# Row-wise scores issued ahead of each burst of narrow products, with three filling products between

## The chip, the cores and the metric

The kernel runs on one core of a Trainium2 chip. The metric is the time of one execution on the device in microseconds (us), the median of several runs. TensorE does the matmuls, ACT (the scalar engine) the exponentials, DVE (the vector engine) the reductions and most copies out of PSUM, POOL (GpSimd) sums between tiles in SBUF, and SP issues the DMAs.

## The reference

Two independent halves, put side by side in the last dimension, all in fp32:

```
A:  q = x @ wq  (32 heads of 32), k = x @ wk, v = x @ wv  (one key and value head for all)
    p = softmax(q k^T / sqrt(32)) for each head, over 2048 keys
    a = concat(p v) @ wo                                   x: [1, 2048, 1024]
B:  y = dft_seq_re @ (x @ dft_hid_re^T) - dft_seq_im @ (x @ dft_hid_im^T)
out = concat([a, y], axis=-1)                              [1, 2048, 2048]
```

## The kernel before

**Two kinds of work in one order.** The 32 heads in groups of four (8 groups) and the 2048 queries in blocks of 512 (4 blocks) make 32 *units* of attention. Everything else, projections, the transform of B in two stages and the output projection, is *fill*: groups of 24 matmuls (12 in the first stage of the transform), each group accumulating one bank of PSUM. Large operands are split into a high and a low part, and each product is made of three matmuls. `take(n)` issues n of these matmuls ("products" below); after each it runs `pump()`, which starts the loads, sums, casts and stores that fall due by the count of fill (`pos["fill"]`).

**Attention by steps.** A unit has SU = 32 steps, so there are 1024 in all. In the main loop step n does two different things for two different units:

- `score_step(n + SU + LEAD)`, 44 steps ahead: `scores(s)` computes 128 queries against 1024 keys (two matmuls into `pss`, two buffers of two banks each), DVE takes the row maximum `nm`; `row_sums(s - 1)` lets ACT take exponentials of the step before, in place, with their row sum. These give each row's maximum and sum. Some steps later `lse_1` to `lse_4` join the halves; `lse_3` transposes them on TensorE (`ident`), and they go into the operands of the next part.
- `expo(n)`: the column-wise scores, 128 keys against two heads' 512 queries (two matmuls into `pst`, which has one buffer of two banks), from which ACT writes the exponentials `p`.

**The burst.** After every eighth step `pv` multiplies the exponentials of the eight steps before with v: 16 narrow products of 32 columns each, one after the other, into one of the two banks that the fill uses too (`psb`); then DVE copies or adds the bank to `ov`. Ahead of a burst and of the transposition `aside()` issues up to five more products where a group of fill has just begun or is about to end. `bank` hands out the two banks in turn.

**What sets the order.** Each engine's instructions keep the program's order. `level(n + 1)` at the end of a step issues as much fill as is owed by then; fill issued by `aside` counts, so the next `level` issues less. PRO = 494 products lie ahead of the loop, FILL = 5472 is the total, and LAST = 24 are held back. Before the change the share of a block of eight steps goes evenly to the seven steps that have no burst:

```
def level(n):
    x = (n // 8 + max(n % 8 - 1, 0) / 7) / (total // 8)
    take(int((FILL - PRO - LAST) * x) + PRO - pos["fill"])
```

In the profile nearly all instructions have the line of the helper that records them (L66), so one goes by tile names: `psb<-rh,mh`, `psb<-rl,mh` and `psb<-rh,ml` are fill, `pss` row-wise scores, `pst` column-wise scores, `psb<-p,v` the burst, `psb<-ident` the transposition.

Of the kernel before, what the change touches and what calls it, by code (L numbers as in the profile page):

```python
# [87 lines left out]
def tile_kernel(ctx: ExitStack, tc, xT, wq, wkv, wo, xbT, wT, cT, out):  # L88
# [50 lines left out]
    class Line:  # L139
# [22 lines left out]
        def pump(self):  # L162
            for k in range(4):
                while self.may(k) and self.items[self.n[k]].due - self.lead[k] <= pos["fill"]:
                    self.step(k)
# [6 lines left out]
    pos = {"fill": 0, "s": 0}  # L172
# [128 lines left out]
    def at(p, f):  # L301
        k = len(later)
        while k and later[k - 1][0] > p:
            k -= 1
        later.insert(k, (p, f))

    def run_later():
        while later and later[0][0] <= pos["fill"]:
            later.pop(0)[1]()
# [8 lines left out]
    def store(to, of, key=None):  # L318
        def go():
            move(sp, to, of)  # L320
            if key:
                ready.add(key)
        soon(go)
# [4 lines left out]
    def bank(name, open_=False):  # L328

        b = 1 - cur["bank"] if cur["bank"] is not None else int(used[1] < used[0])  # L330
        cur["at"] += 1
        used[b] = cur["at"]
        if open_:
            cur["bank"] = b
        return ps_b[b].tile([P, W], F32, name=name)
# [10 lines left out]
    def product(g, ps, j):  # L346
        c, w = divmod(j, 3)
        l, r = g.left[c // 4], g.right[c]
        a = (l.lo if w == 2 else l.hi)[:, c % 4]
        te.matmul(ps[:g.rows], a, r.lo if w == 1 else r.hi, start=j == 0, stop=j == g.n - 1)  # L350

    def take(n):
        for _ in range(n):
            if cur["group"] >= len(groups):
                return
            g = groups[cur["group"]]
            j = pos["fill"] - g.at
            if j == 0:
                cur["ps"] = bank("psb", True)
            if j % 3 == 0:  # L360
                RL.force(g.right[j // 3])
            if j % 12 == 0:
                ML.force(g.left[j // 12])
            product(g, cur["ps"], j)
            pos["fill"] += 1
            if j == g.n - 1:
                cur["group"] += 1
                assert all(hasattr(it, "done") for it in g.ys)
                g.post(cur["ps"])
                cur["at"] += 1  # L370
                used[cur["bank"]] = cur["at"]
                cur["bank"] = None
                if g.ys:
                    at(pos["fill"] + 2 * BEHIND, lambda n=len(g.ys): yused.__setitem__(0, yused[0] + n))
            pump()
            run_later()

    def aside():

        if cur["group"] >= len(groups):  # L380
            return
        g = groups[cur["group"]]
        j = pos["fill"] - g.at
        if 0 < j < 6:
            take(6 - j)
        elif j > g.n - 6:
            take(g.n - j)
# [152 lines left out]
    def wo_set(e):  # L540
        return [Item([(lambda g=g: wo[g * P:(g + 1) * P, e * W:(e + 1) * W], 1)]) for g in range(NG)]
# [40 lines left out]
    SU = 32  # L582
    LEAD = 12
    total = SU * len(units)
# [3 lines left out]
    def open_unit(u):  # L588
        b, g = units[u]
        assert ("q", b, g) in ready  # L590
        q = qsp.tile([P, 4, W], F32R, name="qst")
        gp.memset(q[96:P].bitcast(F32), 0.0)
        for r, src in enumerate((qh_d, ql_d, qh_d)):
            move(sp, q[r * DH:(r + 1) * DH], src[b][g].rearrange("(h d) c -> d h c", d=DH))
        qst[u] = q
        nm[u] = sm.tile([P, 2, NC], F32, name="nm")
        ls[u] = sm.tile([P, 2, NC], F32, name="ls")

    def scores(s):
        u, r = divmod(s, SU)  # L600
        i, j = divmod(r, 2)
        h, t = divmod(i, 4)
        ps = ps_s.tile([P, 2 * W], F32, name="pss")
        for a in range(2):
            k0 = (2 * j + a) * W
            te.matmul(ps[:, a * W:(a + 1) * W], qst[u][:, h, t * P:(t + 1) * P], kst[:, k0:k0 + W], start=True, stop=True)
        dve.tensor_reduce(nm[u][:, j, i:i + 1], ps, axis=AX.X, op=ALU.max, negate=True)
        pend[s] = ps

    def row_sums(s):  # L610
        if s not in pend:
            return
        ps = pend.pop(s)
        u, r = divmod(s, SU)
        i, j = divmod(r, 2)
        act.activation(ps, ps, AF.Exp, bias=nm[u][:, j, i:i + 1], accum_out=ls[u][:, j, i:i + 1])

    def lse_1(u):
        m = sm.tile([P, NC], F32, name="mm")
        d = sm.tile([P, 2, NC], F32, name="md")  # L620
        dve.tensor_tensor(m, nm[u][:, 0], nm[u][:, 1], op=ALU.min)
        for j in range(2):
            dve.tensor_sub(d[:, j], m, nm[u][:, j])
        lse[u] = m, d

    def lse_1b(u):
        act.activation(lse[u][1], lse[u][1], AF.Exp)

    def lse_2(u):
        m, d = lse[u]  # L630
        l = sm.tile([P, NC], F32, name="l")
        m2 = sm.tile([P, 3, NC], F32, name="m2")
        dve.tensor_mul(d, d, ls[u])
        dve.tensor_add(l, d[:, 0], d[:, 1])
        dve.tensor_copy(m2[:, 0].bitcast(F32R), m)
        dve.tensor_sub(m2[:, 1], m, m2[:, 0])
        dve.reciprocal(m2[:, 2], l)
        lse[u] = m2

    def lse_3(u):  # L640
        m2 = lse.pop(u)
        aside()
        pm = bank("psb")
        te.transpose(pm[:3 * NC, :P], m2.rearrange("p a b -> p (a b)"), ident)
        mt = sm.tile([3 * NC, P], F32, name="mt")
        dve.tensor_copy(mt, pm[:3 * NC, :P])
        cur["at"] += 1
        lse[u] = mt

    def lse_4(u):  # L650
        mt = lse.pop(u)
        for a in range(2):
            move(sp, qst[u][96 + a:97 + a].rearrange("o h (t c) -> o (h t) c", c=P), mt[a * NC:(a + 1) * NC])
        sp.dma_start(r_d[u], mt[2 * NC:])
# [16 lines left out]
    def pv(u, k):  # L671

        aside()
        ps = bank("psb")
        for c in range(4 * k, 4 * k + 4):
            for h in range(4):
                te.matmul(ps[h * DH:(h + 1) * DH], v[:, c], pt[u, c, h // 2][:, h % 2], start=c == 4 * k, stop=c == 4 * k + 3)
        if k == 0:
            ov[u] = onp.tile([P, W], F32, name="ov")
            dve.tensor_copy(ov[u], ps)  # L680
        else:
            dve.tensor_add(ov[u], ov[u], ps)
        cur["at"] += 1
        if k == NC // 4 - 1:
            b, g = units[u]
            hi_ = onp.tile([P, W], F32R, name="oh")
            lo_ = onp.tile([P, W], F32R, name="ol")
            lse["out"] = hi_, lo_

            def low():  # L690
                dve.tensor_sub(lo_, ov[u], hi_.bitcast(F32))
                if u + 1 < len(units):
                    store(oh_d[b][g], hi_)
                    store(ol_d[b][g], lo_, ("o", b, g))

            ends.append(lambda: dve.tensor_mul(ov[u], ov[u], rb[u]))
            ends.append(lambda: dve.tensor_copy(hi_, ov[u]))
            ends.append(low)

    def score_step(s):  # L700

        if s < total:
            u, r = divmod(s, SU)
            if r == SU - 6 and u + 1 < len(units):
                open_unit(u + 1)
            scores(s)
        row_sums(s - 1)
        u, e = divmod(s - SU, SU)
        if 0 <= u < len(units):
            if e == 1:  # L710
                lse_1(u)
            elif e == 2:
                lse_1b(u)
            elif e == 3:
                lse_2(u)
            elif e == 5:
                lse_3(u)
            elif e == 7:
                lse_4(u)
# [17 lines left out]
    PRO = pos["fill"]  # L737
    FILL = end[0]
    LAST = 24


    def level(n):
        x = (n // 8 + max(n % 8 - 1, 0) / 7) / (total // 8)
        take(int((FILL - PRO - LAST) * x) + PRO - pos["fill"])

    for n in range(total):
        u, r = divmod(n, SU)
        if n == total - 12:
            w1 = wo_set(1)
            add([o_group(NQ - 1, t, e, ws) for e, ws in ((0, w0), (1, w1)) for t in range(4)])  # L750
        score_step(n + SU + LEAD)
        if ends:
            ends.pop(0)()
        expo(n)
        if r == 16:
            inverse(u)
        if r % 8 == 0 and n:
            pv(*divmod(n // 8 - 1, 4))
        level(n + 1)

# [71 lines left out]
```

## Time and profile before

| | |
|---|---|
| median of 3 runs | 2856.29 us (2856.1 to 2858.78) |
| the profiled execution | 2857.77 us, its span 2856.0 us |
| granted TensorE clock, mean | 0.998 |
| busy share: TensorE, its weight loads, ACT, DVE, POOL | 98%, 67%, 79%, 65%, 42% |
| first and last `pst` matmul | 161.4 and 2794.9 us |
| DMA over the span | 167 GB/s |

The span runs from the first instruction to the last. Busy times of matmuls overlap, and their ends are modelled; starts are what to go by. In rows of the timeline the columns are start, duration (us), engine, line, operation, out<-in, shapes, count of merged instructions and, in brackets, the idle time before it and what ended that. PE is TensorE's matmuls, PEld its weight loads.

### The profile page before, as it was taken

The numbers are of one execution on the slowest core, as the hardware profiler recorded it, in microseconds if no ns is written. First come the engines' busy times: TensorE is split into PE (matmuls) and PEld (weight loads), VectorE is DVE, ScalarE is ACT, GpSimd is POOL, SyncE is SP. The second block draws the span as 40 slices with busy tenths as digits, with TensorE's granted clock in tenths as the row PEclk, the third lists the DMA queues.
The fourth block names the chain that finished last, engine by engine and source line by source line (L and its number), as shares of the span: only waits on it lengthen the run. The fifth ranks groups of instructions, "written<-read, shape, count | busy, mean of one in ns | idle before, by whom it ended". The sixth has DMA issues, their size and how long they took to land.

```text
span 2856.0 us, 40040 instructions
## 1 busy us (share of the span) xinstructions
PE 2798.5 (98%) x13904; PEld 1923.4 (67%) x13904; DVE 1869.8 (65%) x2295; ACT 2242.7 (79%) x3286; POOL 1211.7 (42%) x928
## 2 busy tenths in 40 slices
PE   8999999999999999999999999999999999999999
PEld 5776666767666666766666667666666666666656
DVE  5766666767777777666776676776776676755410
ACT  4688888878788888888788878778888788888751
POOL 1211123554424336555564454775766653520000
PEclk9999999999999999999999999999999999999999
DMA  8965435766576455454452454564555533554445
GB/s 296 297 191 171 148 101 166 236 211 198 186 232 209 164 176 162 148 169 127 150 188 92 126 166 123 178 202 144 174 166 152 180 120 99 163 151 137 126 141 170
DMA packets 315723, 480.84 MB, mean 168 GB/s; under 512 B 33408, under 2 KB 98432, under 8 KB 315520
## 3 DMA queue, kind: packets, MB, share of 16 engines
q1 hardware_dynamic: 315520, 478.28, 53.6%
q8 instruction: 109, 1.79, 0.3%
q14 instruction: 94, 0.77, 0.1%
HBM read 364.12 MB, written 112.98 MB: 167 GB/s over the span
## 4 chain that ended last, share of the span: by engine, by line
PE 84%; DVE 6%; ACT 4%; issue 2%; DMA 2%; POOL 1%; SPq 1%; ACTq 0%; POOLq 0%; DVEq 0%
PE psb L66 53%; PE pst L66 16%; PE pss L66 15%; ACT p L66 2%; DVE nm L66 2%; ACT pss L66 1%; DVE mh L66 1%; DMA r<-s 1%; SPq L66 1%; DVE ov L66 1%; DVE rh L66 1%; POOL m L66 1%; POOL ml L66 0%; DVE md L66 0%; DMA p<-in_xT_dram 0%
## 5 line engine op out<-in xcount | busy, mean ns | idle before, releaser
L66 DVE TENSOR_REDUCE nm<-pss 128x1 f32<-128x1024 f32 x1024 | 1248.6, 1221 | 441.7 <-PE pss L66 439.1
L66 ACT ACTIVATE p<-pst 128x1024 f32<-128x1024 f32 x1024 | 1054.5, 1030 | 401.0 <-PE pst L66 394.0
L66 ACT ACTIVATE pss<-pss,nm 128x1024 f32<-128x1024 f32 x1024 | 1118.2, 1092 | 105.8 <-DVE nm L66 99.0
L66 PE MATMUL psb<-rh,mh 128*128 128x512 f32 (+1 forms) x1852 | 730.6, 394 | 9.6 <-ACT rh L66 7.8
L66 PE MATMUL psb<-rh,ml 128*128 128x512 f32 (+1 forms) x1852 | 730.0, 394 | 0.7 <-POOL ml L66 0.7
L66 PE MATMUL psb<-rl,mh 128*128 128x512 f32 (+1 forms) x1852 | 729.5, 394 | 0.3 <-DVE rl L66 0.3
L66 PE MATMUL pst<-qst,kst 128*128 128x512 f32 x2048 | 662.4, 404 | 22.1 <-ACT p L66 21.1
L66 PE MATMUL pss<-kst,qst 128*128 128x512 f32 x2048 | 657.3, 402 | 10.3 <-ACT pss L66 10.1
L66 POOL TENSOR_TENSOR ml<-m,mh 128x512 fp32r<-128x512 f32 x292 | 383.0, 1312 | 503.1 <-DVE mh L66 272.1
L66 POOL TENSOR_TENSOR rl<-r,rh 128x512 fp32r<-128x512 f32 x214 | 280.8, 1312 | 728.1 <-DVE rh L66 463.7
L66 PEld LDWEIGHTS pss<-kst,qst 128*128 128x128 f32 x2048 | 373.5, 188 | 198.8 <-issue 93.1
L66 PEld LDWEIGHTS pst<-qst,kst 128*128 128x128 f32 x2048 | 367.1, 188 | 161.8 <-ACT p L66 84.3
L66 PE MATMUL psb<-p,v 128*32 128x512 f32 x4096 | 466.0, 595 | 1.7 <-DVE y L66 1.7
L66 PEld LDWEIGHTS psb<-rh,mh 128*128 128x128 f32 (+1 forms) x1852 | 347.1, 187 | 94.9 <-ACT rh L66 8.3
L66 PEld LDWEIGHTS psb<-rl,mh 128*128 128x128 f32 (+1 forms) x1852 | 347.0, 187 | 84.4 <-DVE rl L66 1.5
L66 PEld LDWEIGHTS psb<-rh,ml 128*128 128x128 f32 (+1 forms) x1852 | 347.1, 187 | 84.3 <-POOL ml L66 1.1
L66 PEld LDWEIGHTS psb<-p,v 128*32 128x32 f32 x4096 | 120.0, 109 | 277.7 <-issue 263.8
L66 DVE TENSOR_TENSOR ov<-ov,psb 128x512 f32<-128x512 f32 x96 | 65.9, 686 | 297.6 <-PE psb L66 297.5
L66 POOL TENSOR_TENSOR m<-m,m 128x512 f32<-128x512 f32 x192 | 254.0, 1323 | 12.0 <-DMA m<-in_cT_dram 7.0
L66 POOL TENSOR_TENSOR r<-r,r 128x512 f32<-128x512 f32 x112 | 148.5, 1326 | 221.9 <-DMA r<-in_wT_dram 109.1
L66 ACT ACTIVATION_READ_ACCUMULATOR pss<-pss,nm 128x1 f32 x1024 | 214.3, 209 | 0.0
L66 DVE CAST mh<-m 128x512 fp32r<-128x512 f32 x291 | 178.4, 613 | 20.5 <-POOL m L66 11.4
(66 smaller groups left out, 828.5 us busy)
## 6 DMA issues: line engine op xcount, KB each, us to landing
m<-in_cT_dram SPq DMA_DIRECT2D x384, 256.0 KB, 3.7
r<-s SPq DMA_DIRECT2D x192, 256.0 KB, 4.4
y<-y SPq DMA_DIRECT2D x96, 256.0 KB, 4.5
r<-in_wT_dram SPq DMA_DIRECT2D x80, 256.0 KB, 4.3
m<-in_xbT_dram SPq DMA_DIRECT2D x80, 256.0 KB, 4.6
y<-u SPq DMA_DIRECT2D x80, 256.0 KB, 3.0
qst<-qh SPq DMA_DIRECT2D x64, 256.0 KB, 5.8
s<-y SPq DMA_DIRECT2D x64, 256.0 KB, 2.9
```

What stands on the lines that cost most here:

```text
L66: return lambda *a, **k: self.tc.keep_in_program_order(f(*a, **k))
```

## The change

In every step with a burst (n a multiple of 8, not 0), after `expo(n)`, three products of fill are issued, then the row-wise scores of the next step (s = n + 45) with the row sums of the present one; then comes the burst. The following step finds its scores already asked for and only issues the row sums of them. `level` is rewritten to the new order: of a block's share (w products) the burst's step has three, the step behind it half of what each of the other six has. The opening of a unit stays tied to its step.

```diff
-    def score_step(s):
-
-        if s < total:
+    asked = [0]
+
+    def ask(s):
+
+        if s < total and s == asked[0]:
+            asked[0] += 1
             u, r = divmod(s, SU)
             if r == SU - 6 and u + 1 < len(units):
                 open_unit(u + 1)
             scores(s)
-        row_sums(s - 1)
+            row_sums(s - 1)
+        else:
+            row_sums(min(s, total - 1))
+
+    def score_step(s):
+
+        ask(s)
         u, e = divmod(s - SU, SU)
...
     def level(n):
-        x = (n // 8 + max(n % 8 - 1, 0) / 7) / (total // 8)
-        take(int((FILL - PRO - LAST) * x) + PRO - pos["fill"])
+        w = (FILL - PRO - LAST) / (total // 8)
+        m = n % 8
+        take(int(w * (n // 8) + (3 + (w - 3) * max(m - 1.5, 0) / 6.5 if m else 0)) + PRO - pos["fill"])
...
         if r % 8 == 0 and n:
+            take(3)
+            ask(n + 1 + SU + LEAD)
             pv(*divmod(n // 8 - 1, 4))
         level(n + 1)
```

## The prediction

> **What bounds the kernel now.** I read the page first: busy shares, the chain that ended last, then the groups of TensorE.
>
> ```profile
> PE 2798.5 (98%) x13904; PEld 1923.4 (67%) x13904; DVE 1869.8 (65%) x2295; ACT 2242.7 (79%) x3286; POOL 1211.7 (42%) x928
> ...
> PE 84%; DVE 6%; ACT 4%; issue 2%; DMA 2%; POOL 1%; SPq 1%; ACTq 0%; POOLq 0%; DVEq 0%
> ...
> L66 DVE TENSOR_REDUCE nm<-pss 128x1 f32<-128x1024 f32 x1024 | 1248.6, 1221 | 441.7 <-PE pss L66 439.1
> ...
> L66 PE MATMUL pst<-qst,kst 128*128 128x512 f32 x2048 | 662.4, 404 | 22.1 <-ACT p L66 21.1
> ```
>
> TensorE is busy for 98% of the span and holds 84% of the last chain; ACT at 79% and DVE at 65% have room. So time is won or lost only where TensorE's own order makes it wait. The 404 ns of the last row are a duration and not a pitch: matmuls overlap (the rows below), and a stall shorter than the tail of the one before never shows as idle time. So I went on to the waits, where the weight loads show more of it than the matmuls.
>
> ```profile
> ACT p L66 <- PE pst L66: 394.0, 327, 3.9
> ...
> PEld pst L66 <- ACT p L66: 84.3, 181, 1.5
> ...
> PEld pss L66 <- ACT pss L66: 27.2, 34, 3.7
> ...
> PEld psb L66 <- DVE ov L66: 14.6, 22, 1.9
> ```
>
> pst has one buffer: the column-wise products of step n+1 may not start before the exponential of step n has left it. ACT waits for pst far longer (394.0 us) than pst waits for ACT. To price a wait I read the order of time at a burst, n = 480, with its two following steps.
>
> ```profile
> 1402.84 0.63 PE L66 MATMUL pst<-qst,kst 128*128 128x512 f32 x2
> ...
> 1403.31 0.39 PE L66 MATMUL psb<-rh,ml 128*128 128x512 f32 x1
> ...
> 1403.51 1.02 ACT L66 ACTIVATE p<-pst 128x1024 f32<-128x1024 f32 x1 [2.58 <-PE pst L66]
> 1403.54 0.39 PE L66 MATMUL psb<-rh,mh 128*128 128x512 f32 x1
> ...
> 1404.23 0.39 PE L66 MATMUL psb<-rh,mh 128*128 128x512 f32 x1
> ...
> 1404.46 0.63 PE L66 MATMUL pss<-kst,qst 128*128 128x512 f32 x2
> ...
> 1404.93 0.62 PE L66 MATMUL pst<-qst,kst 128*128 128x512 f32 x2
> ```
>
> One product costs 0.23 us of TensorE (1403.31 to 1403.54; the five from 1403.31 to 1404.46), a pair of scores 0.47 (1404.46 to 1404.93). The exponential ends at 1404.53, and its successor's pst comes at 1404.93: with five products between, nothing waits. Now a burst, n = 424, behind which no product stands, because `aside` had taken five ahead of it to get clear of a group's edge and `level` owed none:
>
> ```profile
> 1253.55 3.64 PE L66 MATMUL psb<-p,v 128*32 128x512 f32 x32
> ...
> 1257.69 0.63 PE L66 MATMUL pst<-qst,kst 128*128 128x512 f32 x2
> ...
> 1258.16 0.62 PE L66 MATMUL pss<-kst,qst 128*128 128x512 f32 x2
> 1258.36 1.02 ACT L66 ACTIVATE p<-pst 128x1024 f32<-128x1024 f32 x1 [3.72 <-PE pst L66]
> ...
> 1259.44 0.30 PEld L66 LDWEIGHTS pst<-qst,kst 128*128 128x128 f32 x2 [1.08 <-ACT p L66]
> 1259.44 0.73 PE L66 MATMUL pst<-qst,kst 128*128 128x512 f32 x2 [0.65 <-ACT p L66]
> ...
> 1260.01 0.39 PE L66 MATMUL psb<-rh,mh 128*128 128x512 f32 x1
> ```
>
> From pst to the next pst there lie 1.75 us here (1257.69 to 1259.44), of which two pairs take 0.93; 0.82 us is wait. So f products between leave a wait of 0.82 - 0.23 f, nothing from four on. Behind a wait the pair itself takes 0.57 (1259.44 to 1260.01) where it takes 0.47 undisturbed: 0.10 more. The case f = 3, n = 504, agrees:
>
> ```profile
> 1464.14 0.73 PE L66 MATMUL pss<-kst,qst 128*128 128x512 f32 x2
> 1464.28 0.69 DVE L66 TENSOR_TENSOR ov<-ov,psb 128x512 f32<-128x512 f32 x1 [3.31 <-PE psb L66]
> ...
> 1465.02 0.29 PE L66 MATMUL psb<-ident,m 128*48 128x128 f32 x1
> ...
> 1466.30 0.63 PE L66 MATMUL pss<-kst,qst 128*128 128x512 f32 x2
> ...
> 1466.89 0.30 PEld L66 LDWEIGHTS pst<-qst,kst 128*128 128x128 f32 x2 [0.40 <-ACT p L66]
> 1466.89 0.73 PE L66 MATMUL pst<-qst,kst 128*128 128x512 f32 x2
> ```
>
> 1466.30 + 0.47 = 1466.77, done at 1466.89: 0.12, against 0.13 by the formula.
>
> **The change part by part.**
>
> *Fill behind the burst.* `level` spreads w = (5472 - 494 - 24)/128 = 38.70 products over eight steps (5472 from the sizes of the groups; 494 = 120 + 66 + 44 x 7). Before: none in the burst's step, 5.53 in each other. After: 3 ahead of the burst, 2.68 in the step behind it, 5.49 in the rest. `aside` still takes up to five ahead of the burst, and `level` deducts them from the step behind. I counted f for the 127 bursts with both formulas and the groups' lengths (24 products, 12 in the first stage of the transform). Before: f = 0, 1, 2, 3 at 8, 13, 14, 12 bursts, four or more at 80. After: f = 0, 1, 2, 3 at 43, 13, 30, 41; never four. Waits before: 8 x 0.82 + 13 x 0.59 + 14 x 0.36 + 12 x 0.13 = 20.8 us at 47 bursts; after: 43 x 0.82 + 13 x 0.59 + 30 x 0.36 + 41 x 0.13 = 59.1 us at all 127. With 0.10 each: 25.5 before, 71.8 after. **+46 us**, on the path, since TensorE has nothing else in its order there. Bounds: +38 (without the 0.10) to +46.
>
> The 0.10 is where the Trainium skill and the trace differ. The load of the waiting pair stands at 1259.44 together with its matmul, not ahead of it. The Trainium skill, "TensorE: Matmul & The Clock Gate", Part 2, Step-by-step, says that TensorE pulls weight loads ahead of matmuls still under way; by that the load would be done within the wait and the term would be 38. The trace does not agree: 84.3 us of these waits stand at the loads.
>
> *The row-wise scores moved.* The pair is the same work (0.47 us) ahead of the burst as behind it, and the pst pair now stands directly behind the burst as the pss pair did: nothing either way. Their row maximum and row sum go into the burst's 3.64 us, where DVE idles (3.31 us at 1464.28) and ACT too. Queues: on ACT, the row sum of n+45 now comes ahead of the exponential of n+1, which can't start before the burst ends anyway; on DVE the row maximum comes ahead of `ov`'s addition, which also waits for the burst. Cover: the burst. If DVE is late, it is ACT's exponential and then pst that are late next. SP and POOL: the opening of a unit falls at s mod 8 = 2, the moved steps at 5, so no DMA or memset moves with them; the transfers and casts that three products set off go 0.7 us earlier, with the products.
>
> *A cover that goes.* Once per unit the transposed statistics (`ident`) come behind a burst and need the other bank, thus `ov`'s addition: above, 1464.28 + 0.69 = 1464.97, done at 1465.02. The pss pair at 1464.14 filled that wait; after, it is ahead of the burst and the transposition still can't come earlier. The row of waits above has 22 loads held by `ov`; by their times 20 are of these 31 places, and 20 x 0.47 = 9.4. Where DVE is behind with its statistics, the moved row maximum (1221 ns) also stands ahead of `ov`, at some three places. Bounds 0 to 18; I take **+10**.
>
> *A new wait ahead of the burst.* The moved scores need a pss buffer, the one that step n's own row sum is leaving. They would come 0.23 + 3 x 0.23 = 0.92 us behind the second pst matmul (which starts 0.39 before the end of its pair's row). A usual burst, n = 488, and a late one, n = 472 (whose row sum starts 0.77 us after pst):
>
> ```profile
> 1417.92 1.09 ACT L66 ACTIVATE pss<-pss,nm 128x1024 f32<-128x1024 f32 x1
> 1418.09 0.30 PEld L66 LDWEIGHTS pst<-qst,kst 128*128 128x128 f32 x2 [0.23 <-ACT p L66]
> 1418.13 0.68 PE L66 MATMUL pst<-qst,kst 128*128 128x512 f32 x2
> ...
> 1418.92 0.21 ACT L66 ACTIVATION_READ_ACCUMULATOR pss<-pss,nm 128x1 f32 x1
> ```
>
> ```profile
> 1376.20 0.62 PE L66 MATMUL pst<-qst,kst 128*128 128x512 f32 x2
> 1376.75 3.64 PE L66 MATMUL psb<-p,v 128*32 128x512 f32 x32
> ...
> 1376.97 1.09 ACT L66 ACTIVATE pss<-pss,nm 128x1024 f32<-128x1024 f32 x1 [1.23 <-DVE md L66]
> 1377.98 0.19 ACT L66 ACTIVATION_READ_ACCUMULATOR pss<-pss,nm 128x1 f32 x1
> ```
>
> The first is free at 1419.13 and wanted at about 1419.35; the second is free at 1378.17 and wanted at 1377.35, 0.8 late, and before the burst covered that. The same comparison at the 122 bursts that have such scores (178.68 to 2687.85) finds 17 late, by 7.2 us together, plus 17 x 0.10: 8.9. If ACT ran 0.2 later at each, 49 would be late, by 16. Bounds 0 to 16; I take **+8**.
>
> *What the head start gives back.* ACT and DVE enter the cycle one row sum ahead. What they could save is what TensorE waits for them elsewhere. In the starved slots a load's idle time is 0.27 above the wait (1.08 against 0.82, 0.40 against 0.13). So of 84.3 us over 181 loads, 47 starved ones hold 20.8 + 47 x 0.27 = 33.5; the other 134 hold 50.8 - 134 x 0.27 = 15; pss for its row sums 27.2 - 34 x 0.27 = 18; 0.10 for each of the 168 another 17: at most 50 us. But early in the cycle ACT is mostly caught up as it is. Here are the third and the seventh step behind the burst of n = 480:
>
> ```profile
> 1407.24 0.63 PE L66 MATMUL pst<-qst,kst 128*128 128x512 f32 x2
> ...
> 1407.91 1.03 ACT L66 ACTIVATE p<-pst 128x1024 f32<-128x1024 f32 x1
> ...
> 1416.05 0.63 PE L66 MATMUL pst<-qst,kst 128*128 128x512 f32 x2
> ...
> 1417.02 1.02 ACT L66 ACTIVATE p<-pst 128x1024 f32<-128x1024 f32 x1
> ```
>
> From pst to its exponential there are 0.67 us in the third step, as where ACT had been idle (1402.84 to 1403.51), and 0.97 in the seventh. The waits build up in the later steps, behind DVE's casts, on which the move has little hold. I take a third: **-16**, bounds -50 to 0.
>
> **Sum.** 46 + 10 + 8 - 16 = +48 us. The profiled execution took 2857.77 us (span 2856.0 and 1.8 around it), 1.5 above the median of 2856.29: 2905.8 there, **2904** as a median. All terms at their good ends: 38 + 0 + 0 - 50 = -12; at their bad ends: 46 + 18 + 16 = +80.
>
> **Rivals.**
> *The head start pays for it.* Place: the fourth to eighth step of each cycle; price: up to 50 us back. For it: these waits exist, and a row maximum per burst leaves the busy stretch. Against it: ACT caught up early in the cycle as it is. It decides from a recovery of about 46 on with the two small costs absent: 2857.8 + 46 - 50 = 2854, as a median 2852, no change; with the term at 38 it is 2844, faster.
> *DVE late within the burst.* ACT works in order, so where the row maximum of n+45 ends after the burst, the exponential of n+1 waits and pst behind it. For it: DVE works in order too, and a cast that waits for its data holds the row maximum behind it. Against it: two row maxima, 2.4 us, have the burst's 3.64 and the 0.47 ahead of it. Nothing recovered and both small costs at their bad ends: 2856.3 + 80 = 2936.
> *The burst's step does not do what it says*: at 43 of 127 bursts the step behind has no product, not half. That is in the count; if the edges of groups fell better and f were 2.68 throughout, the after term would be 127 x (0.82 - 0.62 + 0.10) = 38, and +12.6 instead of +46: about 2871.
>
> **How the numbers follow.** The forecast, +20 to +80, gets 0.80; the head start 0.11 (0.06 for a recovery that reaches faster, 0.05 for none beyond break-even); a late DVE 0.04; the better edges 0.05. Range 2866 to 2934: it holds the forecast and the third rival, and leaves out most of the first. A difference of 0.2% is 5.7 us, about what a measurement of this kernel tells from no change. Faster 0.06, same 0.05, slower 0.89.
>
> **What would show it.** TensorE's loads of pst waiting for ACT's exponential should go from 84.3 us over 181 to some 125 us over 230 or more, all the growth at the second pst pair behind a burst. Loads of pss waiting for ACT grow by some ten places, just ahead of bursts. ACT's wait for pst must not fall by more than it does now per burst. I am wrong if the pst pair comes on time there (the exponential starts earlier than I take it to), or if the waits in the later steps vanish.

## The result and the profile after

The change makes the kernel slower: 2924.01 us median (2922.79 to 2924.75, 5 runs) against 2856.29, a ratio of 1.0235 with a 95% interval of 1.0223 to 1.0247. The forecast was 2904 (2866 to 2934), slower.

The lines of the page and of the waits that answer to those shown of before:

```profile
PE 2819.9 (96%) x13904; PEld 1918.6 (66%) x13904; DVE 1873.1 (64%) x2295; ACT 2259.6 (77%) x3286; POOL 1209.7 (41%) x928
...
PE 81%; ACT 5%; DVE 5%; DMA 3%; issue 3%; POOL 2%; SPq 1%; POOLq 0%; ACTq 0%; DVEq 0%
```

```profile
ACT p L66 <- PE pst L66: 426.0, 442, 5.5
...
PEld pst L66 <- ACT p L66: 140.5, 251, 1.6
...
PEld psb L66 <- DVE ov L66: 40.4, 25, 3.5
...
PEld pss L66 <- ACT pss L66: 28.4, 39, 3.5
```

The counts of instructions are the same, and TensorE, the bound, is busy for less of a longer span. The loads of pst wait for ACT's exponential 140.5 us at 251 places instead of 84.3 at 181; the loads of psb (nearly all of the transposition) wait for `ov` 40.4 us instead of 14.6. The loads of pss waiting for row sums grow only from 34 places to 39. ACT waits longer for pst, too (426.0 us at 442 places instead of 394.0 at 327): at these places ACT stood ready, and it was the pst products that came late.

One burst of the changed kernel, n = 528, in order of time, shows two of the three new waits:

```profile
1551.19 0.63 PE L66 MATMUL pst<-qst,kst 128*128 128x512 f32 x2
...
1552.46 0.20 ACT L66 ACTIVATION_READ_ACCUMULATOR pss<-pss,nm 128x1 f32 x1
...
1552.72 0.73 PE L66 MATMUL pss<-kst,qst 128*128 128x512 f32 x2 [0.21 <-ACT pss L66]
...
1554.07 3.64 PE L66 MATMUL psb<-p,v 128*32 128x512 f32 x32
...
1554.80 1.09 ACT L66 ACTIVATE pss<-pss,nm 128x1024 f32<-128x1024 f32 x1
...
1557.64 0.73 PE L66 MATMUL pst<-qst,kst 128*128 128x512 f32 x2
...
1558.21 0.63 PE L66 MATMUL pss<-kst,qst 128*128 128x512 f32 x2
1558.41 1.02 ACT L66 ACTIVATE p<-pst 128x1024 f32<-128x1024 f32 x1 [2.40 <-PE pst L66]
...
1559.48 0.30 PEld L66 LDWEIGHTS pst<-qst,kst 128*128 128x128 f32 x2 [1.08 <-ACT p L66]
```

The moved scores wait at 1552.72 for a row sum read out at 1552.46 + 0.20, which a burst covered before. The row sums do move into the burst (1554.80), as meant. But behind the burst stands no product here: `aside` had taken three beside the three that are new, and the second pst pair comes at 1559.48, held by an exponential that could not begin before 1558.41. The third new wait is that of the transposition, here at n = 504, where it now stands directly behind the burst:

```profile
1489.41 3.64 PE L66 MATMUL psb<-p,v 128*32 128x512 f32 x32
1493.86 0.29 PE L66 MATMUL psb<-ident,m 128*48 128x128 f32 x1 [0.81 <-DVE ov L66]
```

To place the whole difference I took all starts of TensorE's matmuls in the profiled execution and summed, for each place in the cycle of eight steps, the time between successive starts beyond the undisturbed pitch of that pair (0.23 us as a rule, 0.52 behind a burst). "Later steps" are the third to the eighth behind a burst; the gap within the pair right behind the burst, about 13 us in every kernel, is left out. All values are in us; the last column is the median of the runs, from which the profiled execution differs by up to 6 us (the kernel before, run beside them, had medians from 2856.3 to 2859.6, so ratios are given with each experiment).

| kernel | scores ahead of burst | transposition | second pst pair behind burst | later steps | time |
|---|---|---|---|---|---|
| before | none | 8.4 | 27.8 | 43.5 | 2856.3 |
| the change | 8.8 | 22.0 | 75.3 | 42.2 | 2924.0 |
| fill_only | none | 8.3 | 74.4 | 47.4 | 2910.2 |
| ask_even | 14.2 | 22.0 | 32.1 | 62.8 | 2907.3 |
| ask_bare | 65.9 | 20.0 | 29.6 | 41.2 | 2933.6 |
| late_ident | 15.5 | within next | 74.7 | 51.8 | 2930.7 |
| none_behind | none | 8.4 | 119.1 | 49.1 | 2954.3 |
| spread | none | 6.6 | 2.4 | 49.3 | 2839.6 |
| aligned | none | 7.9 | 2.3 | 47.0 | 2836.0 |
| change_aligned | 6.3 | 19.5 | 55.2 | 45.0 | 2904.8 |
| fill_aligned | none | 8.3 | 52.8 | 47.7 | 2887.3 |
| aligned_ramp | none | 7.7 | 7.4 | 55.6 | 2848.8 |

From before to the change the four columns rise by 8.8 + 13.6 + 47.5 - 1.3 = 68.6 us. The spans differ by 2922.9 - 2856.0 = 66.9.

The granted clock is a part of the small differences. In each profile it falls to a half for stretches of 3.4 us (in late_ident 0.50 from 587.10 to 590.50 us), which by their length cost an estimated 1.7 us each; between the first and the last `pst` there are one before, two in the change, five in ask_even and late_ident, four in aligned_ramp. Without the gaps that touch them the later steps have about 42 us before, 41 in the change and 60 in ask_even, so the large differences in the table do not come from the clock.

### The profile page after: what moved, and what is told of

Same layout as the page of the kernel before. It is cut to its first block, busy times and chain, and to the rows that moved or that the text cites. A ratio compares the mean times of both kernels' runs of the same rounds, so it can differ in the third digit from the quotient of the medians.

```text
span 2922.9 us, 40035 instructions
## 1 busy us (share of the span) xinstructions
PE 2819.9 (96%) x13904; PEld 1918.6 (66%) x13904; DVE 1873.1 (64%) x2295; ACT 2259.6 (77%) x3286; POOL 1209.7 (41%) x928
## 4 chain that ended last, share of the span: by engine, by line
PE 81%; ACT 5%; DVE 5%; DMA 3%; issue 3%; POOL 2%; SPq 1%; POOLq 0%; ACTq 0%; DVEq 0%
PE psb L66 51%; PE pst L66 16%; PE pss L66 14%; ACT p L66 4%; DVE nm L66 2%; ACT pss L66 1%; SPq L66 1%; DMA r<-s 1%; DVE mh L66 1%; DVE rh L66 1%; POOL ml L66 1%; DVE ov L66 1%; POOL m L66 1%; DMA m<-in_wq_dram 0%; DMA p<-in_xT_dram 0%
## 5 line engine op out<-in xcount | busy, mean ns | idle before, releaser
L66 ACT ACTIVATE p<-pst 128x1024 f32<-128x1024 f32 x1024 | 1054.2, 1030 | 430.9 <-PE pst L66 426.0
L66 PE MATMUL pst<-qst,kst 128*128 128x512 f32 x2048 | 680.2, 413 | 47.4 <-ACT p L66 46.4
L66 PE MATMUL pss<-kst,qst 128*128 128x512 f32 x2048 | 645.7, 396 | 13.7 <-ACT pss L66 13.3
L66 PEld LDWEIGHTS pst<-qst,kst 128*128 128x128 f32 x2048 | 354.9, 188 | 279.6 <-ACT p L66 140.5
L66 PEld LDWEIGHTS pss<-kst,qst 128*128 128x128 f32 x2048 | 381.1, 188 | 116.0 <-ACT pss L66 28.4
L66 DVE TENSOR_TENSOR ov<-ov,psb 128x512 f32<-128x512 f32 x96 | 65.9, 687 | 280.0 <-PE psb L66 280.0
L66 DVE CAST mh<-m 128x512 fp32r<-128x512 f32 x291 | 170.4, 585 | 14.9 <-DMA m<-in_wq_dram 6.7
```

The lines of the kernel that those rows point to most:

```text
L66: return lambda *a, **k: self.tc.keep_in_program_order(f(*a, **k))
```

## The experiments

The theory to test: three waits, each with a place of its own (the fill behind the burst, the buffer of the moved scores, the transposition), and no time given back. The first rival: the head start of ACT and DVE gives back a good part. The second: it is the moved scores that cost, and not the fill.

### fill_only: the new shares of fill without the moved scores

```diff
             take(3)
-            ask(n + 1 + SU + LEAD)
             pv(*divmod(n // 8 - 1, 4))
```

> The change without the moved scores: three products ahead of the burst and the new shares of fill, but the scores stay behind the burst. Three waits (fill behind the burst, the transposition's lost cover, the scores' buffer): only the first is left, so TensorE waits 72 us at the second pst pair behind the bursts where it waited 25, and the time is 2856 + 46 to 48 = about 2903. Rival, the head start gives time back in the later steps: this kernel has no head start, so the changed kernel (2924) would be less than 19 us above it, by what is given back. Rival, the moved scores themselves are the cost: 2856 to 2866.

Measured: 2910.19 us, ratio 1.0185 (1.017 to 1.02). Its waits:

```profile
PEld pst L66 <- ACT p L66: 152.2, 266, 1.7
...
PEld pss L66 <- ACT pss L66: 21.1, 29, 2.9
...
PEld psb L66 <- DVE ov L66: 14.5, 21, 1.7
```

The pst row is somewhat higher than in the changed kernel, the other two are about as before. By place the starved pair (the second pst pair behind a burst) costs 74.4, 46.6 more than before. Counted from the kernel before run beside it (2857.1), the total is 5 to 7 us over the expectation; the later steps account for 4 of it. The second rival is out: about four fifths of the loss come without any score being moved.

### ask_even: scores moved, the same fill in all seven steps behind the burst

```diff
-        take(int(w * (n // 8) + (3 + (w - 3) * max(m - 1.5, 0) / 6.5 if m else 0)) + PRO - pos["fill"])
+        take(int(w * (n // 8) + (3 + (w - 3) * max(m - 1, 0) / 7 if m else 0)) + PRO - pos["fill"])
```

> The change with the moved scores and the three products, but the step behind the burst has as much fill as the other six ((w - 3)/7 each). Three waits: the first is nearly back to what it was (29 us by the count of products, against 25.5 before), the other two stay at about 10 and 9: 2856 + 23 = 2879. Rival, a head start that gives back: 2863 or less. Rival, the moved scores are the cost: 2920.

Measured: 2907.3 us, ratio 1.0172 (1.0155 to 1.0189), 28 us over what the theory gave. The starved pair is as expected (32.1, against 27.8 before), so the fill behind the burst does set that wait. What was missed is the later steps: 62.8 us instead of 43.5, and 14.2 instead of 8.8 at the moved scores. The three products ahead of the burst are missing elsewhere: here all seven steps have 5.10 instead of 5.53. The change's half share behind the burst, which costs 47 us there, kept the other six at 5.49, and with them the waits of the later steps as they were. So the two ways of paying for three products ahead of the burst come out within 17 us of each other.

### ask_bare: scores moved directly ahead of the burst, fill as before

```diff
-        take(int(w * (n // 8) + (3 + (w - 3) * max(m - 1.5, 0) / 6.5 if m else 0)) + PRO - pos["fill"])
+        take(int(w * (n // 8) + w * max(m - 1, 0) / 7) + PRO - pos["fill"])
...
-            take(3)
             ask(n + 1 + SU + LEAD)
             pv(*divmod(n // 8 - 1, 4))
```

`level` gives each of the seven steps w/7, as before the change.

> The scores moved ahead of the burst with no products between and the shares of fill as before the change. Three waits: behind the burst as before (nothing added), transposition 10, and the scores now want their buffer 0.69 us earlier than in the changed kernel, late at 121 of 122 bursts by the times of the kernel before, 51 us and 0.10 for each: 2856 + 10 + 63 = 2929, with the waits of pss for ACT's row sums grown by about that. Rival, ACT hands the buffer over in time because nothing else hangs on it, or the wait is given back later: 2866 to 2880.

Measured: 2933.62 us, ratio 1.0268 (1.0253 to 1.0283).

```profile
PEld pss L66 <- ACT pss L66: 103.6, 142, 4.5
...
PEld pst L66 <- ACT p L66: 81.4, 173, 1.5
...
PEld psb L66 <- DVE ov L66: 43.1, 31, 2.7
```

This is what the comparison of row sums and scores in the trace of before gave (63 expected, 65.9 by place): the row of pss goes from 27.2 us at 34 places to 103.6 at 142, and pst stays as it was. It also shows what the three products do in the change: they cover this wait, at a price behind the burst.

### late_ident: the changed kernel, transposition one step later

```diff
-            elif e == 5:
+            elif e == 6:
                 lse_3(u)
```

> The changed kernel with the transposition of the statistics one step later, so that it no longer stands directly behind a burst. Three waits: 10 to 11 us less than the changed kernel, 2913, and the waits of psb for ov's addition (19 us at matmuls, 40 us at loads) gone. Rival, the transposition's wait is given back in the next step: 2924.

Measured: 2930.71 us, ratio 1.0257 (1.0242 to 1.0272): no gain, and 11 us less than the changed kernel is excluded. The 7 us by which it lies above the changed kernel are not shown to be a loss: the granted clock of its runs was 0.994 to 0.997, that of the changed kernel's 0.996 to 0.999.

```profile
PEld pst L66 <- ACT p L66: 139.6, 247, 1.6
...
PEld pss L66 <- ACT pss L66: 40.5, 46, 4.8
...
PEld psb L66 <- DVE ov L66: 1.3, 2, 0.7
```

The wait for `ov` did go (1.3 us). Others took its place: 6.7 us more ahead of the bursts, 9.6 more in the later steps, 3 before the loop. Another 8 us are in the bursts and at their starts, of which the half clock explains about 5 by the estimate above, with three stretches more in this loop than in the changed kernel's. So the total is near the rival's 2924, but by place the time did not come back in the next step alone. The kernel also issues some products elsewhere, since the transposition clears group edges too and now does so at other places. So this run shows that the wait for `ov` can be taken away; it does not show that it is worth its 13.6 us, and that stays open.

### none_behind: no fill owed behind the burst, from the kernel before

```diff
-        x = (n // 8 + max(n % 8 - 1, 0) / 7) / (total // 8)
+        x = (n // 8 + max(n % 8 - 2, 0) / 6) / (total // 8)
```

> The kernel before with no fill owed in the step behind the burst and 6.45 instead of 5.53 products in each of the other six. If the wait is 0.82 - 0.23 f and 0.10, all 127 bursts are starved at f = 0: 117 us against 25.5, and 15 more in the step after where the products ahead of the burst are deducted: +106. If in the later steps fewer products mean more waits (the run with 5.1 products in each step had 20 us more of them), more products mean less: of the 43 us there 20 to 30 go, so 2856 + 76 to 86 = 2932 to 2942. Rival, the later steps' waits have nothing to do with the fill in them: 2962.

Measured: 2954.31 us, ratio 1.0337 (1.0323 to 1.0351). The second pst pair waits 119.1 us, 91.3 more than before; the formula gave 116.8 - 25.5 = 91.3. The third step has 28.0 us (2.4 before, 15 more expected), and the other five later steps 21.1 instead of 41.1, the relief that was expected. The total lies between the two forecasts, since the third step cost 11 more than counted.

### spread: what is owed after a burst, evenly over the seven steps

```diff
+    base = [PRO]
+
     def level(n):
-        x = (n // 8 + max(n % 8 - 1, 0) / 7) / (total // 8)
-        take(int((FILL - PRO - LAST) * x) + PRO - pos["fill"])
+        w = (FILL - PRO - LAST) / (total // 8)
+        m = (n - 1) % 8
+        if m == 0:
+            base[0] = pos["fill"]
+        take(int(base[0] + (w * ((n - 1) // 8 + 1) + PRO - base[0]) * m / 7 + 1e-9) - pos["fill"])
```

> The kernel before, with what is owed after a burst spread evenly over the seven steps, so that what was issued ahead of the burst to clear a group's edge is not taken from the step behind it alone: 4 or 5 products behind every burst, no starved slot. -25 us there. But each later step has 0.24 products less on average, and by the run with 5.1 products these cost: +12. 2843. Rival, the fill of the later steps does not matter: 2831. Rival, the starved slots are given back elsewhere: 2856.

Measured: 2839.64 us, ratio 0.9938 (0.9924 to 0.9951): faster than before. The starved pair falls from 27.8 to 2.4, the later steps rise from 43.5 to 49.3, half of the 12 that was expected.

### aligned: no burst near the edge of a group

```diff
+    def goal(k):
+        p = int((FILL - PRO - LAST) * k / (total // 8)) + PRO
+        if 0 < k < total // 8:
+            while any(0 < p + 0 - g.at < 6 or g.n - 6 < p + 0 - g.at < g.n for g in groups):
+                p += 1
+        return p
+
     def level(n):
-        x = (n // 8 + max(n % 8 - 1, 0) / 7) / (total // 8)
-        take(int((FILL - PRO - LAST) * x) + PRO - pos["fill"])
+        k, m = divmod(n - 1, 8)
+        a, b = goal(k), goal(k + 1)
+        take(a + (b - a) * m // 7 - pos["fill"])
```

> The kernel before, with the ends of the blocks chosen so that no burst falls near a group's edge: nothing is issued ahead of a burst, 4 to 6 products behind each, and 5.53 on average in all seven steps. Starved slots gone at no cost to the later steps: -25, 2831. Rival, the starved slots are given back elsewhere: 2850 to 2856.

Measured: 2835.97 us, ratio 0.9923 (0.9909 to 0.9937), the fastest version here. The steps behind the burst of n = 424, at which the kernel before had no product there, and the waits:

```profile
1244.51 0.73 PE L66 MATMUL pss<-kst,qst 128*128 128x512 f32 x2
1245.08 0.63 PE L66 MATMUL pst<-qst,kst 128*128 128x512 f32 x2
1245.55 0.39 PE L66 MATMUL psb<-rh,mh 128*128 128x512 f32 x1
...
1246.24 0.39 PE L66 MATMUL psb<-rh,mh 128*128 128x512 f32 x1
1246.47 0.62 PE L66 MATMUL pss<-kst,qst 128*128 128x512 f32 x2
1246.93 0.63 PE L66 MATMUL pst<-qst,kst 128*128 128x512 f32 x2
```

```profile
PEld pst L66 <- ACT p L66: 59.0, 150, 1.5
...
PEld pss L66 <- ACT pss L66: 36.3, 43, 4.3
```

Four products behind the burst are enough: 0.47 after the pair at 1246.47 comes the next, with no wait. The 84.3 us of before are 59.0 at 31 fewer places, and by place 25.5 us are gone from the starved pair, the number that the count of products had given. 3.5 of them came back in the later steps.

### change_aligned and fill_aligned: what the moved scores are worth alone

Both have the three products ahead of the burst and 2 or 3 behind each, with aligned bursts (`goal` as in aligned, with p + 3 in place of p + 0):

```diff
     def level(n):
...
+        k, m = divmod(n - 1, 8)
+        a, b = goal(k), goal(k + 1)
+        take(a + 3 + int((b - a - 3) * max(m - 0.5, 0) / 6.5 + 1e-9) - pos["fill"])
```

fill_aligned also leaves the scores behind the burst:

```diff
             take(3)
-            ask(n + 1 + SU + LEAD)
             pv(*divmod(n // 8 - 1, 4))
```

> The changed kernel with the ends of the blocks chosen so that three products ahead of the burst never end near a group's edge: 2 or 3 products behind every burst (93 and 34 times). Starved term 51 us by the formula instead of 72: 2924 - 21 = 2903. Rival, the wait behind the burst is not set by the number of products there: 2924.

> The changed kernel with aligned bursts (change_aligned, 1.0163 of the kernel before), without the moved scores: the same 2 or 3 products behind every burst, so what is left between the two is the moved scores alone. If the head start gives nothing back, they cost what was counted for the transposition and the buffer, about 19 us: 2905 - 19 = 2886. If it gives back the third of 50 us that the prediction took, 3 us: 2902. If it gives back all, this kernel is the slower one: 2930.

Measured: change_aligned 2904.76 us, ratio 1.0163 (1.0149 to 1.0176); fill_aligned 2887.28 us, ratio 1.0105 (1.009 to 1.0121). The first confirms the count: with the edges out of the way the starved pair costs 55.2 instead of 75.3 (51 by the formula, over what is left without starving, 2.3). The waits of the two at the disputed places, first with the moved scores, then without:

```profile
PEld pst L66 <- ACT p L66: 120.8, 239, 2.1
...
PEld psb L66 <- DVE ov L66: 42.7, 31, 2.3
```

```profile
PEld pst L66 <- ACT p L66: 125.2, 244, 2.1
...
PEld psb L66 <- DVE ov L66: 14.4, 21, 1.7
```

The moved scores make the kernel 17.5 us slower where the fill is the same (16.6 by the two ratios). Counted for the transposition and the buffer were 19. By place they cost 6.3 + 11.2 there and 55.2 - 52.8 = 2.4 at the starved pair, and the later steps differ by 47.7 - 45.0 = 2.7 in their favour. The first rival is out: the head start gives back some 3 us.

### aligned_ramp: more fill late in the cycle

```diff
-        take(a + (b - a) * m // 7 - pos["fill"])
+        take(a + int((b - a) * m * (m + 22) / 203 + 1e-9) - pos["fill"])
```

> The aligned version (0.9923 of the kernel before), with fill rising over the seven steps from 4.4 products to 6.7 instead of 5.53 in each. The waits of its fifth to eighth steps, 41 us, come from ACT and DVE falling behind over the cycle; with 0.4 to 1.1 products more in the late steps and 0.4 to 1.1 fewer in the early ones, where nothing waits above four, about half of them go: 2836 - 15 to 20 = 2816 to 2821. Rival, those waits come from single casts that wait for their data, and the fill around them doesn't matter: 2836.

Measured: 2848.78 us, ratio 0.9967 (0.9956 to 0.9978): 13 us slower than aligned. The third and fourth steps went from 5.9 to 18.5 us, the second from 2.3 to 7.4, and the sixth to eighth only from 35.6 to 33.2. The waits moved forward to the steps that were cut and hardly left those that got more. A theory by which a late step's waits follow the fill in that step falls with this run; what starts them stays open. Between the change and ask_even, and between before and none_behind, they fell where the later steps had more fill on average.

## Why the prediction was right

The direction and the main term were right. The point forecast was 20 us low, and the errors did not cancel: all four terms came out above it, by 1.5, 3.6, 0.8 and 14.7 us. The range held because it reached up to 2934.

**The starved slots** carried it: forecast +46, by place +47.5 (75.3 - 27.8), and the same formula, 0.82 - 0.23 f and 0.10 behind a wait, gave none_behind's 91.3 and aligned's -25.5. The lower bound of 38 left out the 0.10, and the runs do not bear that out: the second matmuls of the starved pairs stand 13.9 us beyond the pitch at 127 places (5.4 at 51 before), 0.11 each. By the Trainium skill, "TensorE: Matmul & The Clock Gate", Part 2 (Step-by-step), weight loads are pulled ahead of matmuls under way; at a starved pair the trace does not show it, for the load starts with its matmul (1559.48).

**The transposition**: forecast +10 within 0 to 18; +13.6 by place. That the pss pair had covered it is shown by the rows of n = 504 in both kernels: 0.88 us passed from its start to the transposition before, and now TensorE stands idle there for 0.81. Where DVE was late the moved row maximum came on top, as the upper bound had it: at 2094.26 the transposition had waited 2.56 us for `ov`, and on DVE a row maximum of 1.21 us stood directly ahead of `ov`'s addition.

**The scores' buffer**: forecast +8, measured 8.8, with 16 places late where 17 were counted. Its cover, the three products, was shown by ask_bare.

**What the head start gives back** is the step that failed: forecast -16, measured -1.3 by place. The bound of 50 was real (43.5 us of waits in the later steps), but the third that I took had no row behind it; the row that I did quote, ACT caught up in the third step, pointed to nothing being given back. fill_only and fill_aligned put the gift of the head start at 5 and 3 us. With 0 in place of -16 the same sum is 2920.

**The forecast of the rows**: pst loads 140.5 at 251 against some 125 at 230, the growth at the second pair; pss five more places rather than ten; ACT's wait for pst up and not down.

**The rivals.** The head start that pays for it is out (1.3 us back where it needed about 46). A DVE late within the burst would have made the starved pairs wait longer than the count says; 75.3 against 71.8 leaves it 3.5 us at most. The rival of better edges, at about 2871, comes nearest to change_aligned, at 2904.8, which does not meet its condition: there the mean is 2.27 products (93 twos, 34 threes), not 2.68, and the formula gives 51 us rather than 38. The rest of the distance is mainly the moved scores, 17 us there, where the rival's sum had +2 for them. The 2.68 itself is a slip: half of 5.49 is 2.75, or 2.74 on average with `level`'s rounding. The rival would be at about 2869 by that, and the counts of f, and so the +46, do not use it.

## What to carry to other kernels

Where a single buffer ties two matmuls to one engine between them, count the work that stands in between at each place, one by one: a mean of 5.5 products hid 47 places with too few, and evening those out (aligned) gained 0.8%, while feeding the side engines earlier gained nothing. Work put into a gap comes from somewhere, so ask of each moved piece what its old place covered: here a wait for a buffer, a wait for a bank and the latency of an exponential. A credit that only a bound supports should be entered at the end to which the quoted row points.

## What the runs showed of the hardware that was not expected

With TensorE busy for 96 to 98% of the span, its waits still react to small changes in the length of the steps. Between the change and ask_even, which differ in the shares of fill alone, the later steps go from 5.49 products to 5.10, a tenth of a microsecond less, and their waits rise from 42.2 to 62.8 us. Between before and none_behind they go from 5.53 to 6.45, and the waits of the last five fall from 41.1 to 21.1. ACT was busy for only 76 to 79% of the span in these kernels. Which wait starts the others is not shown.
